# ScalarE normalises half of the first tile, and its transposes go ahead of the first matmul

## The chip, the cores and the metric

One core of one Trainium2 chip runs the kernel. The metric is device time in microseconds (us), the median of several executions; lower is better. (One of the first three executions of the kernel before took 206.22 us, 15% above the fastest, so it counts as slow.)

## The reference, cut to what matters

```python
x = A_x                                     # [1, 2048, 512], bf16
xn = _layernorm(x)                          # (x - mean) / sqrt(var + eps), row by row
return x + ssm(xn) + (silu(xn @ w_gate) * (xn @ w_up)) @ w_down
# ssm: a diagonal complex scan over the 2048 rows, with its own matmuls before and after
```

The 2048 rows are worked off in four chunks of 512, and a chunk in four tiles of 128 rows. Every matmul with `xn` needs it transposed, with the 512 features on the partitions as four K tiles of 128. For chunk 0 TensorE does these transposes itself; for the later chunks DMA does them.

## The kernel before

A list scheduler in the kernel orders VectorE's and ScalarE's work; TensorE's order is the program order. This case concerns only the start: chunk 0's layer norm, its transposes, and the gate matmuls of that chunk, which run in quarters of 128 rows so that they can begin when the first tile is ready.

```python
# loads (SyncE's queue unless "act" is named)
x_load(0); x_load(1)
act_q = [touch (act)];  wg_load("a0", K tiles 0-1, eng="act")
x_load(2)
wg_load("a1", K tile 2, eng="act");  wg_load("a2", K tile 3)
x_load(3)
# ... cut

# VectorE: r = reciprocal, n = normalise a half (256 columns), b = statistics of a half, s = combine (ScalarE then takes the root)
for op, a, h in (("r",0,0), ("n",0,0), ("b",1,0), ("b",1,1), ("s",1,0), ("n",0,1), ("b",2,0),
                 ("r",1,0), ("n",1,0), ("n",1,1), ("b",2,1), ("s",2,0), ("b",3,0), ...):   # cut

def xt_tile_fine(a, h):          # transposes of tile a, half h: two of 128 columns
    slot = xt_pair[0]            # always the same PSUM bank
    ...                          # TensorE transposes into the bank; then one evacuation of 256 columns:
    t = g.add("act", activation(out=xnT[half h], in_=bank, Identity))    # VectorE for tile 3

# TensorE (seven gate tiles of 128 columns, one bank each)
pe_warm(9, 512, wbank); pe_warm(2, 128, wbank)
xt_tile_fine(0, 0)
pe_warm(2, 256, wbank)
for q in range(4):
    for k0, k1 in ((0, 2), (2, 3), (3, 4)) if q == 0 else ((0, 2), (2, 4)):
        for n, (i, bk) in enumerate(tiles):
            if k0 == 0 and n == (2 if q == 0 else 1):
                xt_tile_fine(q, 1)
            if k0 == 2 and n == 1 and q < 3:
                xt_tile_fine(q + 1, 0)
            matmuls of K tiles k0..k1 of gate tile i for quarter q
```

I call the transposes of tile 1's first half T10, of tile 0's second half T01, and so on.

## Time and profile before

| | before |
|---|---|
| time | 179.57 us, median of the first 3, and of the 5 fast ones of 6 |
| TensorE busy (engine table) | 98% of a span of 177.8 us |
| VectorE busy | 92% |
| ScalarE busy | 49% |
| first gate matmul (timeline) | 5.81 us |
| first matmul of 512 columns, where the quarters are done | 13.20 us |

Part 1 of the page gives the busy time of each engine, and part 4 the chain of work that ended last:

```profile
PE 173.5 (98%) x928; PEld 83.8 (47%) x936; DVE 163.1 (92%) x285; ACT 87.5 (49%) x110; POOL 9.2 (5%) x21
...
PE 95%; DMA 1%; DVE 1%; issue 0%; ACT 0%
```

TensorE bounds the kernel, so VectorE's 92% is no limit by itself. What can be won must be time in which TensorE does no useful matmul. The timeline of TensorE shows where that is. Its columns are start, duration, engine, line, operation, what is written and read, shapes, how many; a bracket tells of idle time before.

```profile
4.96 0.28 PE L569 MATMUL pb<-ident,xn_sb 128*128 128x128 bf16 x2 [0.35 <-DVE xn_sb L514]
5.08 0.38 PE L474 MATMUL pb<-const-bfloat16-1.0 128*128 128x256 bf16 x2
5.81 0.38 PE L785 MATMUL pb<-xnT,wg 128*128 128x128 bf16 x4 [0.34 <-ACT xnT L581]
6.07 0.29 PE L569 MATMUL pb<-ident,xn_sb 128*128 128x128 bf16 x2
6.20 0.87 PE L785 MATMUL pb<-xnT,wg 128*128 128x128 bf16 x11
6.90 0.27 PE L569 MATMUL pb<-ident,xn_sb 128*128 128x128 bf16 x2
7.01 1.00 PE L785 MATMUL pb<-xnT,wg 128*128 128x128 bf16 x15
7.85 0.28 PE L569 MATMUL pb<-ident,xn_sb 128*128 128x128 bf16 x2
...
13.20 1.03 PE L743 MATMUL pb<-xnT,wg 128*128 128x512 bf16 x4
```

L569 are the transposes and L785 the gate matmuls; L474 are dummy matmuls that keep the array busy. A gate matmul is issued every 56 ns, yet each is drawn with about 219 ns, because they are pipelined. So a short wait does not appear as a gap between two bars: one has to look at the distance between two starts. T01 itself starts 0.101 us after the matmul before it, 0.045 us too late, at 6.07: VectorE's half was ready at 6.01. The eleventh gate matmul after T01 starts 0.137 us after the one before it, 0.08 us too late, at 6.83.

ScalarE's timeline at the same place shows the evacuations (L581) and the square roots (L521):

```profile
4.03 0.29 ACT L521 ACTIVATE sd<-mv,epst 128x1 f32<-128x1 f32 x1 [0.20 <-DVE mv L519]
5.28 0.38 ACT L581 ACTIVATE xnT<-pb 128x256 bf16<-128x256 bf16 x1 [0.96 <-PE pb L569]
5.84 0.29 ACT L521 ACTIVATE sd<-mv,epst 128x1 f32<-128x1 f32 x1 [0.18 <-DVE mv L519]
6.39 0.38 ACT L581 ACTIVATE xnT<-pb 128x256 bf16<-128x256 bf16 x1 [0.26 <-PE pb L569]
7.21 0.38 ACT L581 ACTIVATE xnT<-pb 128x256 bf16<-128x256 bf16 x1 [0.43 <-PE pb L569]
```

One round trip can be read from the two together: T10 starts at 6.90, its evacuation at 7.21, ends at 7.59, and its first matmul may start about 0.05 later. That is about 0.75 us. Thirteen gate matmuls and the two transposes fill it (15 x 0.056 = 0.84 us), so TensorE never notices.

### The profile page before, as it was taken

What the parts mean: (1) busy time and instruction counts of PE and PEld (TensorE: products, weight loads), DVE (VectorE), ACT (ScalarE), POOL (GpSimd) and SP (SyncE); (2) the same over time, 40 slices, a digit from 0 to 9 for tenths busy, and PEclk for the clock granted to TensorE, in tenths of its full rate; (3) what the DMA queues carried; (4) which work ended last, traced back from release to release, by engine and by line L of the source; (5) the groups of instructions that cost most, each with busy time, mean ns of one, the idle gap of its engine ahead of it and who ended that gap; (6) DMA issues with size and microseconds to landing.
All of it is one profiled execution on the core that took longest, in us unless ns stands there. A gap on an engine that the chain in (4) does not pass through costs nothing.

```text
span 177.8 us, 2415 instructions
## 1 busy us (share of the span) xinstructions
PE 173.5 (98%) x928; PEld 83.8 (47%) x936; DVE 163.1 (92%) x285; ACT 87.5 (49%) x110; POOL 9.2 (5%) x21
## 2 busy tenths in 40 slices
PE   8899999999999999999999999999999999999994
PEld 3794444444444444444444444444444444444743
DVE  2968998997999999999999999999899999999933
ACT  4469989699999674043565660000965520000000
POOL 3013300210000000300000000000000000000000
PEclk9999999999999999999999999999999999999999
DMA  5995563569540000012600000002000000001022
GB/s 168 375 332 118 120 122 118 118 137 331 156 82 0 0 0 0 0 33 87 122 0 0 0 0 4 0 30 82 7 0 4 0 0 0 0 0 54 9 89 89
DMA packets 22978, 12.37 MB, mean 70 GB/s; under 512 B 15192, under 2 KB 22968, under 8 KB 22968
## 3 DMA queue, kind: packets, MB, share of 16 engines
q1 hardware_dynamic: 22472, 11.54, 23.5%
q10 hardware_dynamic: 496, 0.69, 1.1%
q8 instruction: 7, 0.11, 0.3%
q14 instruction: 3, 0.02, 0.0%
HBM read 6.46 MB, written 2.10 MB: 48 GB/s over the span
## 4 chain that ended last, share of the span: by engine, by line
PE 95%; DMA 1%; DVE 1%; issue 0%; ACT 0%
PE pb L743 36%; PE pb L940 21%; PE pb L857 16%; PE pb L953 15%; PE pb L785 4%; PE pb L820 2%; DMA x_sb<-in_A_x_dram 1%; PE pb L830 1%; PE pb L569 1%; DVE st L527 0%; ACT xnT L581 0%; DVE xn_sb L514 0%; ACT sd L521 0%; DVE x_sb L958 0%; DVE mv L519 0%
## 5 line engine op out<-in xcount | busy, mean ns | idle before, releaser
L897 DVE TENSOR_TENSOR_SCAN rot<-sm,car,rot 128x512 bf16<-128x512 f32 x32 | 39.0, 1267 | 0.1
L940 PE MATMUL pb<-wd,hT 128*128 128x512 bf16 (+3 forms) x194 | 38.1, 355 | 0.2
L743 PE MATMUL pb<-xnT,wu 128*128 128x512 bf16 x160 | 37.3, 379 | 0.0
L743 PE MATMUL pb<-xnT,wg 128*128 128x512 bf16 x132 | 31.3, 379 | 0.0
L953 PE MATMUL pb<-W,hss 128*128 128x512 bf16 (+2 forms) x140 | 28.1, 355 | 0.2
L857 PE MATMUL pb<-xnT,BT 128*128 128x512 bf16 x128 | 28.1, 379 | 0.0
L940 PEld LDWEIGHTS pb<-wd,hT 128*128 128x128 bf16 (+1 forms) x198 | 18.5, 98 | 19.9
L755 ACT ACTIVATE sg<-pb 128x1024 bf16<-128x1024 f32 x20 | 20.1, 1024 | 9.4 <-PE pb L743 8.2
L743 PEld LDWEIGHTS pb<-xnT,wu 128*128 128x128 bf16 x160 | 15.6, 98 | 18.9 <-issue 0.2
L810 ACT ACTIVATE uf<-pb 128x1024 bf16<-128x1024 f32 x20 | 20.6, 1028 | 7.4 <-PE pb L743 6.0
L953 PEld LDWEIGHTS pb<-W,hss 128*128 128x128 bf16 x144 | 13.5, 98 | 14.3
L743 PEld LDWEIGHTS pb<-xnT,wg 128*128 128x128 bf16 x132 | 12.7, 98 | 15.7 <-issue 0.8
L857 PEld LDWEIGHTS pb<-xnT,BT 128*128 128x128 bf16 x128 | 12.5, 98 | 15.1
L864 ACT ACTIVATE u_sb<-pb 128x1024 bf16<-128x1024 f32 x16 | 16.2, 1021 | 6.1 <-PE pb L857 5.7
L958 DVE TENSOR_TENSOR x_sb<-pb,x_sb 128x512 bf16<-128x512 f32 (+2 forms) x18 | 11.1, 623 | 3.6 <-PE pb L953 3.5
L812 DVE TENSOR_TENSOR hT<-sg,uf 128x1024 bf16<-128x1024 bf16 x20 | 13.4, 682 | 0.3 <-ACT uf L810 0.3
L503 ACT ACTIVATE xn_sb<-x_sb,nmr,rstd 128x512 bf16<-128x512 bf16 x8 | 6.0, 803 | 9.2 <-DVE nmr L500 9.2
L839 ACT ACTIVATE sg<-pb 96x1024 bf16<-96x1024 f32 x2 | 2.0, 1019 | 17.1 <-PE pb L820 17.1
L888 DVE TENSOR_TENSOR rot<-u_sb,cosT 128x2048 bf16<-128x2048 bf16 x8 | 9.7, 1218 | 0.3 <-ACT u_sb L864 0.3
L888 DVE TENSOR_TENSOR rot<-rot,cosT 128x2048 bf16<-128x2048 bf16 x8 | 9.7, 1215 | 0.1
L888 DVE TENSOR_TENSOR rot<-u_sb,sin 128x2048 bf16<-128x2048 bf16 x8 | 9.7, 1218 | 0.0
L888 DVE TENSOR_TENSOR rot<-rot,sin 128x2048 bf16<-128x2048 bf16 x8 | 9.7, 1216 | 0.0
(78 smaller groups left out, 140.2 us busy)
## 6 DMA issues: line engine op xcount, KB each, us to landing
out_dram<-x_sb SPq DMA_DIRECT2D x15, 128.0 KB, 1.7
x_sb<-in_A_x_dram SPq DMA_DIRECT2D x3, 512.0 KB, 6.8
wd<-in_B_w_down_dram SPq DMA_DIRECT2D x1, 1280.0 KB, 6.2
wu<-in_B_w_up_dram SPq DMA_DIRECT2D x1, 768.0 KB, 5.1
wu<-in_B_w_up_dram SPq DMA_DIRECT2D x1, 608.0 KB, 7.2
x_sb<-in_A_x_dram SPq DMA_DIRECT2D x4, 128.0 KB, 3.4
wg<-in_B_w_gate_dram SPq DMA_DIRECT2D x1, 480.0 KB, 6.1
wg<-in_B_w_gate_dram ACTq DMA_DIRECT2D x1, 448.0 KB, 3.8
```

The source lines that it names most:

```text
L743: inst = e.matmul(pbank[0:fs, bk, :].rearrange("p (j t) -> p j t", j=4), lhsT=w[:, kt, i * 128:i * 128 + fs], rhs=xnT[:, c % 2, :, kt, :], ...
L755: g.add("act", lambda e: e.activation(out=sg[rows, sl, 0:n, :].rearrange("p a t -> p (a t)"), in_=pair_f32(rows, bk, 512 * n), func=AF.Sil ...
L785: inst = e.matmul(pbank[:, bk, q * 128:(q + 1) * 128], lhsT=wg[:, kt, i * 128:(i + 1) * 128], rhs=xnT[:, 0, q, kt, :], start=(kt == 0), st ...
L810: g.add("act", lambda e: e.activation(out=uf[rows, ul, 0:n, :].rearrange("p a t -> p (a t)"), in_=pair_f32(rows, bk, 512 * n), func=AF.Ide ...
L812: g.add("dve", lambda e: e.tensor_tensor(out=hT[rows, hb, i0:i0 + n, :], in0=sg[rows, sl, 0:n, :], in1=uf[rows, ul, 0:n, :], op=ALU.mult), ...
L857: inst = e.matmul(pbank[:, bk, :].rearrange("p (j t) -> p j t", j=4), lhsT=BT[:, ri, kt, pt * 128:(pt + 1) * 128], rhs=xnT[:, c % 2, :, kt ...
L864: g.add("act", lambda e: e.activation(out=u_sb[:, us].rearrange("p r t -> p (r t)"), in_=pair_f32(slice(0, 128), b0), func=AF.Identity), r ...
L888: tt = lambda out, a, b, op, r, w, nm: g.add("dve", lambda e: e.tensor_tensor(out=out, in0=a, in1=b, op=op), reads=r, writes=w, name="%s_% ...
L897: g.add("dve", lambda e, A0=A0, A1=A1, k=k, ri=ri, pt=pt: e.tensor_tensor_scan(out=A1[:, k, ri, :], data0=rr[:, pt:pt + 1].to_broadcast([1 ...
L940: inst = e.matmul(pbank[:, bk, 0:nc_], lhsT=hT[0:fs, hb, i, lt * 128:(lt + 1) * 128], rhs=wd[0:fs, i, c0:c0 + nc_], start=(i == 0), stop=F ...
L953: inst = e.matmul(pbank[:, bk, 0:nc_], lhsT=hss[:, hb, pt, ri, lt * 128:(lt + 1) * 128], rhs=W12[:, ri, pt, c0:c0 + nc_], start=False, sto ...
L958: g.add("dve", lambda e, bk=bk, a=a, c0=c0, nc_=nc_: e.tensor_tensor(out=x_sb[:, a, c0:c0 + nc_], in0=pbank[:, bk, 0:nc_], in1=x_sb[:, a, ...
```

## The change

The intent: the first gate matmul starts 0.85 us after the first transposes, and the transposes of tile 0's second half stand in the middle of the gate matmuls because VectorE normalises that half late (at 5.72). ScalarE is idle there, so it takes that half. Its transposes then go ahead of the first gate matmul, into another PSUM bank, and the first evacuation is cut in two so that K tile 0 can start early.

```diff
+ negm0 = ScalarE: -mean                       # before the reciprocal is there
+ nmr0  = ScalarE: negm0 * rstd
+ xn[0, 256:512] = ScalarE: Identity(rstd * x + nmr0)
- ("s",1,0), ("n",0,1), ("b",2,0),             # VectorE
+ ("s",1,0), ("b",2,0),
...
+ elif a == 0 and h == 0:                      # first evacuation: two of 128 columns
+     for j in range(2):
+         ScalarE: xnT[:, j] <- bank[:, j]
...
-            xt_tile_fine(0, 0)
-            pe_warm(2, 256, wbank)
+            xt_tile_fine(0, 0, wbank)
+            pe_warm(1, 256, tiles[-2][1])
+            xt_tile_fine(0, 1)
+            pe_warm(1, 256, tiles[-2][1])
             for q in range(4):
-                for k0, k1 in ((0, 2), (2, 3), (3, 4)) if q == 0 else ((0, 2), (2, 4)):
+                for k0, k1 in ((0, 1), (1, 2), (2, 3), (3, 4)) if q == 0 else ((0, 2), (2, 4)):
                     for n, (i, bk) in enumerate(tiles):
-                        if k0 == 0 and n == (2 if q == 0 else 1):
+                        if k0 == 0 and n == 1 and q:
                             xt_tile_fine(q, 1)
-                        if k0 == 2 and n == 1 and q < 3:
+                        if k0 == (2 if q else 3) and n == (0, 2, 1, 9)[q]:
                             xt_tile_fine(q + 1, 0)
...
-            seq = ["sd0", "ev00", "sd1", "ev01", "ev10", ...]                # ScalarE's order
+            seq = ["sd0", "negm0", "nmr0", "xa01", "ev0a", "ev00", "sd1", "ev01", "ev10", ...]
```

The `(0, 2, 1, 9)` line moves T10 from after the first K-tile-2 matmul of quarter 0 to before the first K-tile-3 matmul, and T20 to one gate tile later.

More of the change, by code (lines that the diff above doesn't have):

```diff
@@ L326, in bass_parallel_sum__ssm_conv_s5__swiglu_ffn__prompt_kernel @@
         rstd = sb("rstd", [128, NT], F32)
+        nm0 = sb("nm0", [128, 2], F32)
         nmr = sb("nmr", [128, NT], F32)
@@ L531, in ln_chunk0 @@
             last = ln_stat0(0, (bn_full(0),))
-            for op, a, h in (("r", 0, 0), ("n", 0, 0), ("b", 1, 0), ("b", 1, 1), ("s", 1, 0), ("n", 0, 1), ("b", 2, 0),
+            g.add("act", lambda e: e.activation(out=nm0[:, 0:1], in_=mv[:, 0, 0:1], func=AF.Identity, scale=-1.0), reads=[("mv", 0)], writes=[("nm0", 0)],
+                  name="negm0", est=220, order=(hold["sd0"],))
+            hold["negm0"] = g.tasks[-1]
+            for op, a, h in (("r", 0, 0), ("n", 0, 0), ("b", 1, 0), ("b", 1, 1), ("s", 1, 0), ("b", 2, 0),
                              ("r", 1, 0), ("n", 1, 0), ("n", 1, 1), ("b", 2, 1), ("s", 2, 0), ("b", 3, 0),
@@ L537, in ln_chunk0 @@
                     last = recip(a, (last,))
+                    if a == 0:
+                        g.add("act", lambda e: e.activation(out=nm0[:, 1:2], in_=nm0[:, 0:1], func=AF.Identity, scale=rstd[:, 0:1]),
+                              reads=[("nm0", 0), ("rstd", 0)], writes=[("nm0", 1)], name="nmr0", est=290)
+                        hold["nmr0"] = g.tasks[-1]
+                        g.add("act", lambda e: e.activation(out=xn_sb[:, 0, 256:512], in_=x_sb[:, 0, 256:512], func=AF.Identity, bias=nm0[:, 1:2], scale=rstd[:, 0:1]),
+                              reads=[("x", 0), ("rstd", 0), ("nm0", 1)], writes=[("xh", 0, 1)], name="xn0_1", est=430)
+                        hold["xa01"] = g.tasks[-1]
                 elif op == "n":
@@ L558, in bass_parallel_sum__ssm_conv_s5__swiglu_ffn__prompt_kernel, with xt_tile_fine @@
         xt_pair = [None]
-        def xt_tile_fine(a, h):
-            slot = xt_pair[0]
+        def xt_tile_fine(a, h, slot=None):
+            slot = xt_pair[0] if slot is None else slot
             par = a == 3 and h == 1
@@ L579, in xt_tile_fine @@
                           reads=BK(slot), writes=[("praw", k) for k in range(3)], name="parTev", est=80, order=(t,))
+            elif a == 0 and h == 0:
+                for j in range(2):
+                    t = g.add("act", lambda e, j=j: e.activation(out=dst[:, j], in_=src[:, j], func=AF.Identity), reads=BK(slot), writes=[("xnTq", j)],
+                              name="xTev0_0%d" % j, est=240, order=(t,) if j else ())
+                    if j == 0:
+                        hold["ev0a"] = t
             else:
@@ L787, in mm @@
                             return inst
-                        g.add("pe", mm, reads=[("wg", "a%d" % max(k - 1, 0)) for k in range(k0, k1)] + [("xnTh", q, k0 // 2)], writes=BK(bk), name="mm_gq%d_%d_%d" % (i, q, k0),
+                        g.add("pe", mm, reads=[("wg", "a%d" % max(k - 1, 0)) for k in range(k0, k1)] + ([("xnTq", k0)] if q == 0 and k0 < 2 else [("xnTh", q, k0 // 2)]), writes=BK(bk), name="mm_gq%d_%d_%d" % (i, q, k0),
                               est=(k1 - k0) * 56, ninst=k1 - k0)
             reserved.clear()
-            seq = ["sd0", "ev00", "sd1", "ev01", "ev10", "sd2", "ev11", "ev20", "sd3", "ev21"]
+            seq = ["sd0", "negm0", "nmr0", "xa01", "ev0a", "ev00", "sd1", "ev01", "ev10", "sd2", "ev11", "ev20", "sd3", "ev21"]
             for a_, b_ in zip(seq, seq[1:]):
```

## The prediction

> **What bounds the kernel now.** TensorE. The profile's engine table has PE busy 98% of the 177.8 us span, and the chain that ended last is 95% PE. Listing PE's instructions in order of time, I find that from the first gate matmul (5.81 us) to the end matmuls start one every 56 ns (128 columns) or 216 ns (512 columns); the only waits in the first 14 us after that start are about 0.08 us at 6.70 (for the evacuation of tile 0's second half) and 0.1 us at 11.4. DVE (92% busy) has slack: the last scan output is ready at 165.6 us, its first reader starts at 168.3. The clock is full. So only the first 8 us matter: every 0.1 us that PE's stream of quarter matmuls ends earlier or later comes out 1:1 at the end.
>
> **The start before (timeline).** x lands 3.06; statistics, sqrt, reciprocal to 4.52; DVE normalises half 0 to 4.90; transposes 4.96; ScalarE evacuates 5.28-5.66 (383 ns); first matmul 5.81. Half 1 is normalised only at 5.72-6.01, transposed inside the matmul stream at 6.07, evacuated to 6.78.
>
> **What changes.** ScalarE gets negm0, nmr0 and xn0_1; DVE loses one 294 ns half; the 383 ns evacuation becomes two of 128 columns. Costs: ScalarE, the Trainium skill, "ScalarE: Activation LUTs", section "What ACT_TABLE_LOAD costs", gives 186 ns + 0.833 ns per column, 93 ns per pointer operand, about 93 ns overlap back to back. The trace agrees: 638 ns for 512 columns, 734 with one pointer, 803 with two, 294 for 128x1 with one. Estimates: negm0 0.2, nmr0 0.29, xn0_1 0.59, each 128-column evacuation 0.28 us.
>
> Walking it forward: negm0 4.23-4.42; nmr0 waits for rstd, 4.55-4.84; xn0_1 4.88-5.46 (0.55 us earlier than DVE had it); but the first evacuation now queues behind it: 5.37-5.65, the second half to 5.83. So the first K tile is ready when both were before. PE: half-1 transposes at about 5.52, one warm matmul, first gate matmul about 5.75 (before 5.81). sd1 keeps 5.84-6.13; half 1's evacuation 6.04-6.42, in time for K tile 2 at 6.53, so the 0.08 us wait goes, and one pair of transposes (0.11 us) is ahead of the stream.
>
> Given back: tile 1's first transposes now stand before K tile 3's seven matmuls, at about 6.92. Before, from transposes' start to the matmul that may use them took 0.32 + 0.38 + 0.06 = 0.76 us, covered by 13 matmuls. Now only 0.11 + 7x0.056 = 0.50 us covers it: a new wait of about 0.26 us. Quarter 1 starts at about 7.68 (before 7.74). In quarter 1 tile 2's transposes move one tile later, 10 matmuls cover 0.67 of 0.76 us: another 0.09 us. Net about zero: -0.06 + 0.09. Everything later is unchanged in PE's order; DVE and ScalarE may be re-ordered by the list scheduler, but they have slack of over 2 us.
>
> **Predicted time:** 179.55 us (before 179.57), 8 in 10 within 179.2 to 179.9. Faster by over 2%: 0.01; within 2%: 0.98; slower: 0.01.
>
> **What would show it.** Timeline: first gate matmul between 5.65 and 5.9; xn0_1 about 0.58 us on ScalarE, ending about 5.46; first 128-column evacuation starting after it, not at 5.28; a PE gap of about 0.25 us before quarter 1's first matmul waiting for ScalarE, and about 0.1 us before quarter 2's; then the chain identical, shifted by under 0.2 us.
>
> **What would make it wrong.** If ScalarE reaches the first evacuation at 5.28 after all, or the transposes' round trip is shorter than 0.76 us, the gain is up to 0.3 us. If xn0_1 or the semaphore waits between dependent ScalarE operations cost more, the start slips by as much. A re-ordering that makes DVE late for the gate-up products or tables could cost more than all of this.

## The result

The changed kernel took 179.69 us (median of 6, 179.6 to 180.1) against 179.57. A ratio in this document is the mean time of one kernel's fast runs over that of the other's of the same rounds, so it is not quite the ratio of the medians quoted beside it. Here it is 1.0008, 95% interval 0.9994 to 1.0021: the same. Executions over 1.5% slower than the fastest of the same kernel are left out of the means.

The page's two lines, as above:

```profile
PE 173.9 (98%) x936; PEld 83.7 (47%) x936; DVE 163.1 (92%) x284; ACT 88.3 (50%) x114; POOL 9.2 (5%) x21
...
PE 95%; DMA 1%; ACT 1%; DVE 1%; issue 0%
```

TensorE still holds 95% of the chain. The page cannot tell the two kernels apart; the start of TensorE's timeline can (L580 transposes, L804 gate matmuls, L475 dummies):

```profile
4.96 0.29 PE L580 MATMUL pb<-ident,xn_sb 128*128 128x128 bf16 x2 [0.51 <-DVE xn_sb L515]
5.08 0.27 PE L475 MATMUL pb<-const-bfloat16-1.0 128*128 128x256 bf16 x1
5.53 0.29 PE L580 MATMUL pb<-ident,xn_sb 128*128 128x128 bf16 x2 [0.18 <-ACT xn_sb L546]
5.66 0.27 PE L475 MATMUL pb<-const-bfloat16-1.0 128*128 128x256 bf16 x1
5.76 1.33 PE L804 MATMUL pb<-xnT,wg 128*128 128x128 bf16 x21
6.94 0.28 PE L580 MATMUL pb<-ident,xn_sb 128*128 128x128 bf16 x2
7.05 0.93 PE L804 MATMUL pb<-xnT,wg 128*128 128x128 bf16 x9
7.81 0.28 PE L580 MATMUL pb<-ident,xn_sb 128*128 128x128 bf16 x2
...
13.26 1.03 PE L760 MATMUL pb<-xnT,wg 128*128 128x512 bf16 x4
```

T01 has gone from 6.07 to 5.53, ahead of the first gate matmul, which starts at 5.76 in place of 5.81. What that one waits for is no longer ScalarE but the dummy matmul ahead of it: it was issued at 5.655, and two such dummies start 0.109 apart in the trace before. The first piece of the evacuation was done at 5.64, and 0.056 later would be 5.70, so by this estimate the dummy costs some 0.07 us; no run takes it out. Twenty-one gate matmuls follow without a stop. The line of nine at 7.05 is the telling one: nine matmuls at 56 ns take 0.50 us, but the next transposes start 0.76 us later. Seven of the nine are quarter 0's last; then TensorE stands still until T10 has come back through ScalarE. By single starts, the seventh is at 7.383 and quarter 1's first at 7.690: 0.307 apart, a wait of 0.25 us. Before quarter 2 there is another, 0.138 in place of 0.056, so 0.08 us.

ScalarE's timeline (L533 and L543 the two small scalars, L546 the normalisation, L593 and L598 evacuations):

```profile
4.02 0.29 ACT L522 ACTIVATE sd<-mv,epst 128x1 f32<-128x1 f32 x1 [0.20 <-DVE mv L520]
4.22 0.19 ACT L533 ACTIVATE nm<-mv 128x1 f32<-128x1 f32 x1
4.55 0.29 ACT L543 ACTIVATE nm<-nm,rstd 128x1 f32<-128x1 f32 x1
4.88 0.60 ACT L546 ACTIVATE xn_sb<-x_sb,nm,rstd 128x256 bf16<-128x256 bf16 x1
5.38 0.42 ACT L593 ACTIVATE xnT<-pb 128x128 bf16<-128x128 bf16 x2
...
6.04 0.36 ACT L598 ACTIVATE xnT<-pb 128x256 bf16<-128x256 bf16 x1
7.25 0.38 ACT L598 ACTIVATE xnT<-pb 128x256 bf16<-128x256 bf16 x1 [0.85 <-PE pb L580]
```

The first evacuation was due at 5.28 (the transposes are done at 5.24) but starts at 5.38, behind the normalisation; its first half is done at 5.64, where the whole was done at 5.66 before.

These are the marks of TensorE's stream, from the starts of single matmuls:

| | before | after | moved by |
|---|---|---|---|
| first gate matmul | 5.806 | 5.765 | -0.041 |
| quarter 1's first | 7.737 | 7.690 | -0.047 |
| quarter 2's first | 9.524 | 9.568 | +0.044 |
| first of 512 columns | 13.200 | 13.255 | +0.055 |
| last addition of the chain | 175.48 | 175.53 | +0.05 |

ScalarE's order is the same after the start. VectorE's is the same but for the operation removed and one small one (128x4), which the scheduler moved from 28.69 to 17.61 us. It had no effect: from the first matmul of 512 columns to the last addition the kernels take 162.28 and 162.27 us.

### The profile page after: what moved, and what is told of

Read it like the earlier page. It is cut to its first block, busy times and chain, and to the rows that moved or that the text cites. A ratio compares the mean times of both kernels' runs of the same rounds, so it can differ in the third digit from the quotient of the medians.

```text
span 177.8 us, 2427 instructions
## 1 busy us (share of the span) xinstructions
PE 173.9 (98%) x936; PEld 83.7 (47%) x936; DVE 163.1 (92%) x284; ACT 88.3 (50%) x114; POOL 9.2 (5%) x21
## 4 chain that ended last, share of the span: by engine, by line
PE 95%; DMA 1%; ACT 1%; DVE 1%; issue 0%
PE pb L760 36%; PE pb L959 21%; PE pb L972 16%; PE pb L876 16%; PE pb L804 3%; PE pb L839 2%; DMA x_sb<-in_A_x_dram 1%; PE pb L849 1%; PE pb L580 1%; DVE st L528 0%; ACT xn_sb L546 0%; ACT xnT L598 0%; ACT sd L522 0%; ACT nm L543 0%; DVE x_sb L977 0%
## 5 line engine op out<-in xcount | busy, mean ns | idle before, releaser
L959 PE MATMUL pb<-wd,hT 128*128 128x512 bf16 (+3 forms) x198 | 38.8, 355 | 0.0
```

The lines of the kernel that those rows point to most:

```text
L959: inst = e.matmul(pbank[:, bk, 0:nc_], lhsT=hT[0:fs, hb, i, lt * 128:(lt + 1) * 128], rhs=wd[0:fs, i, c0:c0 + nc_], start=(i == 0), stop=F ...
```

## The experiments

My theory: TensorE's stream of quarter matmuls sets the time 1:1. The change wins one pair of transposes, the 0.08 us wait and a slightly earlier start, and its own placement of T10 and T20 gives that back as two new waits. The rivals: later stages absorb the start; tile 1's statistics, and not the placement, hold up quarter 1; one part of the change pays alone and another takes it away.

The table has the marks from each profile. "root 0" is the start of ScalarE's first square root, which moves with the landing of tile 0 of x (3.94 to 4.13 in these profiles) and shifts everything after it; "x2" is the landing of tile 2 of x. Times are medians, with that of the kernel before; e0 to e3, e4 to e6, e7 to e10, e11 ran on four different chips. By the rule of 2% every run is "the same"; the argument rests on the traces first.

| run | root 0 | x2 | first gate | first of 512 | last addition | time | before |
|---|---|---|---|---|---|---|---|
| before | 4.03 | 5.43 | 5.81 | 13.20 | 175.48 | 179.57 | |
| after | 4.02 | 5.56 | 5.77 | 13.26 | 175.53 | 179.69 | 179.57 |
| e0_after | 4.10 | 5.48 | 5.84 | 13.33 | 175.61 | 179.72 | 179.73 |
| e1_place | 4.02 | 6.02 | 5.76 | 13.20 | 175.48 | 179.50 | 179.73 |
| e2_whole | 4.10 | 5.88 | 6.01 | 13.77 | 176.04 | 179.78 | 179.73 |
| e3_dose | 4.12 | 6.44 | 6.31 | 13.79 | 176.07 | 180.11 | 179.73 |
| e4_onebank | 4.04 | 5.41 | 6.11 | 13.60 | 175.87 | 179.95 | 179.69 |
| e5_actnorm | 4.08 | 5.88 | 5.95 | 13.36 | 175.64 | 179.72 | 179.69 |
| e6_split | 4.05 | 6.08 | 5.73 | 13.34 | 175.62 | 179.65 | 179.69 |
| e7_place2 | 4.06 | 6.02 | 5.80 | 13.21 | 175.48 | 179.48 | 179.68 |
| e8_load | 3.94 | 5.42 | 5.68 | 12.92 | 175.20 | 179.40 | 179.68 |
| e9_whole2 | 4.10 | 5.99 | 5.88 | 13.78 | 176.05 | 180.09 | 179.68 |
| e10_latex2 | 4.13 | 6.66 | 5.87 | 13.85 | 176.12 | 180.35 | 179.68 |
| e11_loadonly | 4.04 | 5.77 | 5.78 | 13.27 | 175.54 | 179.68 | 179.68 |

Last addition minus first of 512 is 162.27 to 162.28 us in all fourteen profiles. Nothing after 13 us took part in any of these differences. The times follow the same mark: the time of each profiled execution, less its own first matmul of 512 columns, is 166.31 to 166.36 us in all fourteen. So an execution without a profile can be placed by its time alone, as an estimate good to about 0.03 us.

### The changed kernel again (e0_after)

No edit.

> The changed kernel again, beside its variants. Theory (the new waits give back what the moved transposes save): as its first profile; first gate matmul 5.77 us, waits of 0.25 us at 7.38 and 0.08 us at 9.43, first 512-column matmul at 13.26 (before 13.20), time 179.6 to 179.8, ratio to before 1.000 to 1.001. Rival (the small difference is noise): ratio anywhere within 0.999 to 1.001 and no fixed shift of 0.05 us in the trace.

Measured: 179.72 us, ratio to before 1.0002 (0.999 to 1.0014). The waits were 0.25 us at 7.46 and 0.08 us at 9.51, and every mark stood 0.075 us later than in the first profile, as tile 0 of x did. The pattern is fixed and the position floats with the first landing. The 0.055 us is thus in both traces of the changed kernel, but too small for the times to show.

### A dose of delay (e3_dose)

```diff
             xt_tile_fine(0, 1)
-            pe_warm(1, 256, tiles[-2][1])
+            pe_warm(5, 256, tiles[-2][1])
```

> The changed kernel with four more warm matmuls of 256 columns before the first gate matmul: a delay of 4 x 0.109 = 0.43 us put into PE's stream alone. My theory (every 0.1 us of the quarter stream comes out 1:1 at the end): first gate matmul 6.20, first 512-column matmul at 13.69, time 180.1, ratio to the changed kernel 1.0024. Rival (slack later, or the wait before quarter 1, absorbs it): 0 to 0.2 us in time. The wait of 0.25 us before quarter 1 should stay, because it starts from PE's own transposes, not from a fixed time.

Its timeline of TensorE:

```profile
5.75 0.72 PE L475 MATMUL pb<-const-bfloat16-1.0 128*128 128x256 bf16 x5
6.31 1.33 PE L804 MATMUL pb<-xnT,wg 128*128 128x128 bf16 x21
...
13.79 1.03 PE L760 MATMUL pb<-xnT,wg 128*128 128x512 bf16 x4
```

The first gate matmul came 0.54 us after the changed kernel's, of which 0.10 was tile 0 of x and 0.44 the dose; the first matmul of 512 columns came 0.54 later, and the last addition too. The time was 180.11 us, 0.39 above the changed kernel beside it, ratio to before 1.0017 (1.0005 to 1.0029). The wait before quarter 1 stayed at 0.25 us. The profiled executions themselves took 180.11 and 179.60, 0.51 apart. So later stages absorb nothing, and that rival falls. The wait moves with TensorE's own transposes.

### The transposes moved up (e1_place, e7_place2)

```diff
-                        if k0 == (2 if q else 3) and n == (0, 2, 1, 9)[q]:
+                        if k0 == 2 and n == (3, 1, 1, 9)[q]:
```

> The changed kernel with tile 1's first transposes moved up by 11 matmuls (into K tile 2, before its fourth matmul) and tile 2's back by one matmul tile, so that more matmuls cover the trip through ScalarE. My theory: the waits of 0.25 us before quarter 1 and 0.08 us before quarter 2 shrink to under 0.08 in total; quarter 1 starts at about 7.52 (limit: tile 1's normalised half lands at 6.71, plus 0.05 and the 0.75 us trip), first 512-column matmul at about 13.00, time about 179.43, 0.25 us under the changed kernel and 0.13 under before. Rival 1 (quarter 1 waits for tile 1's statistics, not for the placement): quarter 1 still starts at 7.69 and nothing is won. Rival 2 (later stages absorb the start): stream ends early at 13.00 but the time stays 179.69.

Measured: 179.50 us against 179.72 for the changed kernel and 179.73 for the one before; ratio to before 0.9982 (0.997 to 0.9994). The time is where my theory put it, but the profile is not. Quarter 1 started at 7.73 and not at 7.52. The two old waits are gone, all but 0.03 us, and a new one of 0.26 us stands before T10 itself. In VectorE's timeline of this run its cause is in brackets:

```profile
5.59 0.21 DVE L520 BATCH_NORM_AGGREGATE mv<-st 128x2 f32<-128x12 f32 x1
6.04 0.43 DVE L510 BATCH_NORM_STATS2 st<-x_sb 128x6 f32<-128x256 bf16 x1 [0.24 <-DMA x_sb<-in_A_x_dram]
6.38 0.15 DVE L530 RECIPROCAL rstd<-sd 128x1 f32<-128x1 f32 x1
6.57 0.60 DVE L515 TENSOR_SCALAR xn_sb<-x_sb,mv,rstd 128x256 bf16<-128x256 bf16 x2
```

The statistics of tile 2 (6.04) stand ahead of tile 1's reciprocal and normalisation in VectorE's order, and tile 2 of x landed at 6.02. In the changed kernel's profile it had landed at 5.56, in time. So rival 1, that tile 1's statistics hold up quarter 1, is false for the changed kernel but true as soon as the placement is mended and tile 2 is late. I ran the same kernel again to see if that was chance.

> The same kernel as the one with the transposes moved up, once more. In its first profile tile 2 of x landed at 6.02 (5.4 to 5.6 in the profiles of before and of the changed kernel); VectorE, in order, stood waiting for it with tile 1's reciprocal behind it, so tile 1's half was ready at 6.91 and PE waited 0.26 us for it. Theory now: the gain depends on that landing. If x tile 2 lands by 5.7: first 512-column matmul about 13.00; for each 0.1 us later, 0.1 us later, up to about 13.26. Time again about 0.2 us under the changed kernel's, 179.4 to 179.6.

Measured: 179.48 us against 179.68 before, ratio 0.9993 (0.998 to 1.0006); one of its six runs took 180.1. Tile 2 landed at 6.02 again, and the trace repeats: quarter 1 at 7.73. So the medians were about 0.2 us better in both, the ratio was clear of 1 in one of two, and its profile never showed the full gain.

### Tile 2 of x on purpose late, and early (e10_latex2, e8_load, e11_loadonly)

Late, on top of the moved transposes:

```diff
-        x_load(2)
         act_q.append(wg_load("a1", 2, 3, eng="act", ...))
         wg_load("a2", 3, 4)
+        x_load(2)
         x_load(3)
```

> The kernel with the transposes moved up, with tile 2 of x on purpose issued behind all gate weights. Theory (VectorE's order ties tile 1's normalisation to tile 2's landing): x tile 2 lands at about 6.5 to 7.0, statistics of tile 2 start right there, tile 1's half is ready 0.87 us after that landing (7.4 to 7.9), quarter 1 starts 0.8 us after that, first 512-column matmul 13.7 to 14.3, time +0.7 to +1.2 us. Rival (tile 1 does not hang on tile 2's load): no change of 13.0 to 13.2.

In the chain that ended last (start, duration, what), tile 2's load now leads straight to tile 1's transposes:

```profile
2.18 4.48 DMA x_sb<-in_A_x_dram
...
6.69 0.43 DVE st L510
7.11 0.07 DVE rstd L530
...
7.21 0.36 DVE xn_sb L515
...
7.62 0.29 PE pb L580 x2
```

Tile 1's half was ready at 7.56, 0.90 us after tile 2 of x had landed (6.66), the first matmul of 512 columns came at 13.85, and the time was 180.35 us, 0.67 above before, just under the 0.7 I had named. VectorE's program order ties one tile's normalisation to the next tile's load.

Early: the weights of K tile 2 were issued from ScalarE's queue at the same moment (1.71) as tile 2 of x. The Trainium skill ("DMA: Bandwidth & Descriptors", section "Issuing engines are not separate DMA queues") says that DMAs of different issuers run on the same 16 engines and interleave; whether that is what delayed tile 2, no run here shows (see the caution under e11_loadonly). To try it, I issued those weights after tile 2 of x, on SyncE's queue, again on top of the moved transposes:

```diff
-        act_q.append(wg_load("a1", 2, 3, eng="act", order=(act_q[-1],)))
+        wg_load("a1", 2, 3)
```

> The same with one load moved: the third K tile of the gate weights is issued from the queue of SyncE behind tile 2 of x, not beside it from ScalarE's. Theory: x tile 2 lands before 5.5, VectorE's statistics of tile 2 start at 5.72 unhindered, tile 1's half is ready at 6.71, quarter 1 starts at about 7.52, first 512-column matmul at about 13.00 (each mark moves with x tile 0's landing, by up to 0.08); the third K tile's weights land later than now, 6.1 to 6.5, still before 6.55 where they are needed. Time 179.3 to 179.45. Rival (the load order makes no difference to the landing): as the run beside it, with waits for x tile 2 or, new, for weights.

TensorE's timeline of that run:

```profile
5.68 1.11 PE L804 MATMUL pb<-xnT,wg 128*128 128x128 bf16 x17
6.69 0.28 PE L580 MATMUL pb<-ident,xn_sb 128*128 128x128 bf16 x2
6.81 0.92 PE L804 MATMUL pb<-xnT,wg 128*128 128x128 bf16 x13
7.57 0.28 PE L580 MATMUL pb<-ident,xn_sb 128*128 128x128 bf16 x2
...
12.92 1.03 PE L760 MATMUL pb<-xnT,wg 128*128 128x512 bf16 x4
```

Tile 2 landed at 5.42 and the weights at 6.19. Eleven of the 13 matmuls after T10 are quarter 0's and, with the two transposes, cover its trip all but 0.03 us (13 x 0.056 = 0.73 us; from T10 at 6.69 to quarter 1's first at 7.45 are 0.76). Before T10 there is a wait of 0.06 us for tile 1's half. The first matmul of 512 columns is at 12.92; tile 0 of x was 0.08 us early in this run, so on the changed kernel's clock it is 13.00, as forecast. The time was 179.40 us against 179.68, ratio 0.9987 (0.9975 to 0.9999). It has the lowest median of all the kernels, though its interval overlaps that of e1_place and of e11_loadonly below.

The load order alone, with the change's own placement:

> The changed kernel with the moved weight load alone, its transposes where the change put them. Theory (the placement is what gives the gain back; the load order only lets the better placement work): quarter 1 still starts 1.93 us after the first gate matmul, with the wait of about 0.25 us before it and 0.08 before quarter 2; first 512-column matmul 13.17 to 13.33 (x tile 0's landing moves it), time 179.6 to 179.75, ratio to before 0.999 to 1.001. Rival (the load order alone gives the gain of the run before): first 512-column matmul at about 13.0 and time about 179.4.

```profile
6.95 0.28 PE L580 MATMUL pb<-ident,xn_sb 128*128 128x128 bf16 x2
7.07 0.92 PE L804 MATMUL pb<-xnT,wg 128*128 128x128 bf16 x9
7.83 0.28 PE L580 MATMUL pb<-ident,xn_sb 128*128 128x128 bf16 x2
...
13.27 1.03 PE L760 MATMUL pb<-xnT,wg 128*128 128x512 bf16 x4
```

Measured: waits of 0.25 and 0.08 us as in the changed kernel, first matmul of 512 columns at 13.27, 179.68 us, ratio 1.0003 (0.9989 to 1.0016). None of its five executions took less than 179.61 us. The load order alone gives nothing, and the placement is what gave the gain back. One caution: tile 2 landed at 5.77 here and at 5.41 to 5.56 in four profiles with the old load order, so two profiles do not show that the new order makes it land early.

### The parts of the change one by one (e5_actnorm, e6_split, e4_onebank, e2_whole, e9_whole2)

**Only ScalarE's normalisation** on the kernel before: transposes, banks and evacuations untouched.

```diff
+ negm0, nmr0, xn[0, 256:512] on ScalarE          (as in the change)
- ("n",0,1) on VectorE
- seq = ["sd0", "ev00", ...]
+ seq = ["sd0", "negm0", "nmr0", "xa01", "ev00", ...]
```

> The kernel before with only the first part of the change: ScalarE normalises tile 0's second half; transposes, banks and evacuations as before. My theory: the evacuation queues behind the normalisation (5.38 to 5.77 instead of 5.28 to 5.66), first gate matmul 5.83 to 5.91 (before 5.81), the 0.08 us wait for the second half stays since it is set by the 10 matmuls that cover the trip; first 512-column matmul 13.20 to 13.30, so no gain. Rival (relieving VectorE pays by itself, as tile 1's statistics come sooner): first 512-column matmul at 13.1 or earlier.

Measured: 179.72 against 179.69, ratio 1.0 (0.9985 to 1.0015). First gate matmul at 5.95 with tile 0 of x 0.06 late, so 5.89; first of 512 at 13.36, so 13.30. No gain, as expected, at the upper end of my figure: the wait for the second half's evacuation was 0.17 and not 0.08 us. The difference is as large as the 0.09 us that the last section finds for how the wait is issued.

**Only the split** of the first evacuation by K tile, on the kernel before, with T01 before K tile 1's matmuls.

```diff
- for k0, k1 in ((0, 2), (2, 3), (3, 4)) if q == 0 ...
+ for k0, k1 in ((0, 1), (1, 2), (2, 3), (3, 4)) if q == 0 ...
- if k0 == 0 and n == (2 if q == 0 else 1):
+ if (k0, n) == ((1, 0) if q == 0 else (0, 1)):
+ first evacuation in two pieces                  (as in the change)
```

> The kernel before with only the split of the first evacuation by K tile: VectorE still normalises tile 0's second half (ready 6.01), its transposes stand before K tile 1's matmuls. My theory: first piece 5.28 to 5.54, first gate matmul 5.60 to 5.70 (before 5.81), but K tile 2 still needs the second half's evacuation, which ends at about 6.78 as before, so a wait of about 0.25 us opens before it and the first 512-column matmul stays within 0.06 of 13.20. Rival (an earlier first matmul is what counts): first 512-column matmul at about 13.08.

Measured: the first gate matmul went to 5.73 (5.70, the end of my band, with tile 0's landing taken off) and a wait of 0.25 us opened before K tile 2, as expected. The first of 512 missed my band: 13.34, or 13.32 with tile 0's landing taken off. A second wait of 0.11 us before T10 came on top, because tile 2 of x landed at 6.08 and held tile 1's normalisation to 6.98. Without that wait it would be 13.21. The time, 179.65 against 179.69, ratio 0.9994 (0.9979 to 1.0009), is the same. An earlier first matmul by itself is worth nothing here.

**One bank** for both halves of tile 0 again:

```diff
-            xt_tile_fine(0, 0, wbank)
+            xt_tile_fine(0, 0)
```

> The changed kernel with tile 0's two transposes in one PSUM bank again, order unchanged. My theory: the second pair must wait for the end of the first half's evacuation (5.81), so it runs at about 5.86 and holds up the first gate matmul behind it in PE's order: first gate matmul 6.09, first 512-column matmul at about 13.58 (+0.32 us), time about 180.0. Rival (the bank does not matter since ScalarE's normalisation is late anyway): first gate matmul stays at 5.77.

TensorE's timeline names the wait:

```profile
5.88 0.29 PE L580 MATMUL pb<-ident,xn_sb 128*128 128x128 bf16 x2 [0.51 <-ACT xnT L593]
...
6.11 1.34 PE L804 MATMUL pb<-xnT,wg 128*128 128x128 bf16 x21
```

T01 waits for the evacuation of T00 out of the bank. The first of 512 came at 13.60 and the time was 179.95 against 179.69, ratio 1.0018 (1.0002 to 1.0035). With the transposes in front, the second bank is worth about 0.33 us (13.60 less 13.26, less 0.02 for tile 0's landing); it is needed for the new order, not a gain over the old one.

**The evacuation whole** again in the changed kernel:

```diff
- first evacuation in two pieces; K tiles 0 and 1 each wait for their own
+ first evacuation in one piece of 256 columns; both wait for it
```

> The changed kernel with the first evacuation in one piece of 256 columns again. My theory: evacuation 5.38 to 5.77 behind ScalarE's normalisation, first gate matmul 5.82 instead of 5.77, all later marks +0.06 us, first 512-column matmul at 13.31, time +0.06. Rival (the split is what pays): the first matmul would slip by a whole evacuation, 0.15 us or more.

The time, 179.78 against 179.72 for the changed kernel beside it, fits the 0.06 us of my theory, which is less than these runs resolve (ratio to before 1.0003, 0.9991 to 1.0015). The profile fits nothing: first of 512 at 13.77. TensorE ran its first matmuls at 107 ns each; the last slow one started at 6.43. I profiled it again.

> The changed kernel with the whole first evacuation, profiled again, because in its first profile PE ran its first gate matmuls at 107 ns each until 6.43 (in the others it had gone over to 56 ns by 5.2). Theory: with PE fast from 5.2 on, first gate matmul 5.82 to 5.90 and first 512-column matmul 13.31 (plus up to 0.08 with x tile 0's landing); the 13.77 of the first profile was PE's rate. Rival: 13.6 or later again, so the whole evacuation itself costs it.

This time TensorE was fast, and the first gate matmul came at 5.88, 5.80 on the changed kernel's clock: 0.04 us later, where I had said 0.06. But the weights of K tile 2 landed at 7.02 (5.93 to 6.67 in the other profiles with this load order), and TensorE stood 0.39 us for them; first of 512 at 13.78, one run of 180.09 us. So 13.6 or later did come again, and yet not from the evacuation: the cause was another each time. With the 0.39 and tile 0's 0.08 taken off, 13.78 is 13.31, the figure of my theory; that is a subtraction and not a run. The split's worth is shown for the first matmul (0.04 us, with the dummy in front of it), not for the end.

## Why the prediction was right

Inside the range, and nearly every mark of the walk was met to 0.02 us.

- **TensorE alone bounds, 1:1 from the start.** Shown: 162.27 to 162.28 us remain after the quarters in all fourteen profiles, and a dose of 0.44 us came out whole in the trace (0.39 in the medians).
- **The first evacuation queues behind the normalisation.** Predicted 4.88 to 5.46 for the normalisation and 5.37 to 5.65 for the first piece; measured 4.88 to 5.48 and 5.38 to 5.64. My estimate from the Trainium skill's cost of an ACTIVATE ("ScalarE: Activation LUTs", section "What ACT_TABLE_LOAD costs") was 0.585 us for 256 columns and two pointers; the trace has 0.60.
- **First gate matmul 5.75, quarter 1 at 7.68.** Measured 5.765 and 7.690. The old wait of 0.08 us went, as predicted.
- **Two new waits of 0.26 and 0.09 us.** Measured 0.25 and 0.08. That they come from the placement is shown by e1_place, e7_place2 and e8_load, which take them away to within 0.03 us, and by e11_loadonly, which keeps the placement and them. In e1_place and e7_place2 a wait for tile 1's half took their place; e8_load alone shows the gain in its trace.
- **Net about zero.** My terms summed to +0.03 us; TensorE's stream came out at +0.055. I nevertheless named 179.55, 0.02 below before: the sum should have given 179.60. The measured median is 179.69, and 179.72 beside a before of 179.73. I had also missed the old wait of 0.045 us before T01. It moved none of my marks, since I walked forward from T10, but only with it does the account close: -0.04 (start), -0.11 (transposes), -0.08 and -0.045 (old waits), +0.25 and +0.08 (new waits) make +0.055.
- **How much the range tests.** A range of 0.7 us about the old time would also have held if nothing at all had changed. What tests the mechanism is the marks and the two waits.
- **What I had left out.** I treated the loads as fixed times. Between profiles tile 2 of x landed anywhere from 5.41 to 6.08 (6.44 in e3_dose) in kernels that do not move its load, and TensorE went over to its fast rate anywhere from about 3.5 (e8_load) to 6.5 us (e2_whole). Both can cost more in a single run than the change moves.
- **What would have made it wrong.** A re-ordering did happen, of one small operation of VectorE, and cost nothing. I did not see the slack of later stages used up in any run.

What stays open: whether the load order of e8_load makes tile 2 land early reliably, or that one profile was lucky; and how often the unprofiled runs had a late tile 2. Their times place the first matmul of 512 columns of e1_place and e7_place2 at 12.96 to 13.77 (an estimate: their times less 166.33 us, the middle of the range above), but do not say which landing was late.

## What to carry to other kernels

When transposed data goes from TensorE through another engine and back, count the matmuls that stand between the transposes and their first user, and compare their time with the round trip (here 0.75 us from the transposes' start: the two transposes and 11 to 12 matmuls of 56 ns). Moving work ahead of the first matmul pays only if the next round trip stays covered; seven matmuls cost 0.25 us of waiting here, which used up the whole gain. And on an engine that works in order, see what stands ahead of the critical operation: tile 2's statistics in front of tile 1's reciprocal made a load that looked two steps away set the pace.

## What the Trainium skill lacked or had wrong

- "Perfetto Trace Analysis", section "Identifying Dependency Chains", says that an instruction with several waits may have extra EventSemaphore instructions before it, and gives no cost. Where the wait that ends last sat in such an instruction and the weight load behind it carried another, long met wait, TensorE started 0.145 us after ScalarE's end (5.661 to 5.806 before; 5.586 to 5.732 in e6_split; 5.802 to 5.947 in e5_actnorm); where it sat on the weight load itself, 0.056 us (6.778 to 6.834 before). That is 0.09 us for the order of the waits.
- "TensorE: Matmul & The Clock Gate", section "What you observe", puts the passage from 107 to 56 ns at about 4 us of activity, plus or minus 0.5. The two rates agree. In these profiles, with the first dummy matmul at 0.83 us, the passage came from about 2.7 us after it (e8_load; 2.9 in the changed kernel) to 5.7 us after it (e2_whole, between the starts at 6.435 and 6.541, with short waits between). The granted clock in the result of that run is still 1.0, so the rate has to be read from the starts of the matmuls.
- "ScalarE: Activation LUTs", section "What ACT_TABLE_LOAD costs": 186 ns plus 0.833 ns per column, stated without a word on where the tile lies, would give 293 ns for an evacuation of 128 columns from PSUM without pointers, and 399 for 256 (estimates); the traces have 255 to 277 for the pieces, and 363 to 385 for 256 columns.
- No page that I found gives the spread of a load's landing from run to run. The same 128 KB load, issued at 1.71 us, landed between 5.41 and 6.44 us.
